# Sliding-window attention and a hardswish layer on one core: batch 0's q and k of pair 1 loaded as f32 by SP, pairs 2 and 3 two to an issue, and all of its V by POOL's casting queue

## The chip, the core and the metric

The kernel runs on one core of one Trainium2 chip. The core has TensorE (PE in the profile, with PEld for its weight loads), VectorE (DVE), ScalarE (ACT), GpSimd (POOL) and SyncE (SP), and 16 DMA engines that are shared by the queues of SP and POOL. The metric is the device time of one execution in microseconds, lower is better. Comparisons are made between runs on the same chip.

## What is computed

Attention over 8 batches, 8 heads, 576 positions and a head dimension of 64, in which each position sees itself and the 63 positions before it; then a two-matrix layer over the 4,608 tokens with a hardswish between:

```python
scores = scale * np.matmul(q, k.transpose(0, 1, 3, 2))
rel = pos[:, None] - pos[None, :]
mask = (rel >= 0) & (rel < 64)
scores = np.where(mask, scores, -1000000000.0)
attn = softmax(scores)                  # over the last axis
x = np.matmul(attn, v).transpose(0, 2, 1, 3).reshape(4608, 512)
h = x @ w_in                            # 512 -> 2048
g = h * np.clip(h + 3.0, 0.0, 6.0) / 6.0
out = g @ w_out                         # 2048 -> 512
```

Inputs and output are f32 in DRAM; the kernel computes on TensorE in bf16 with f32 sums.

## The kernel before

**Tiling.** Heads go in four pairs g = 0 to 3 (two heads of 64 fill 128 partitions). Queries go in blocks of 64; each sees 128 keys, and so V is kept in blocks of 128 rows in two alignments: blocks 0 to 3 (`NE = 4`) at multiples of 128, and blocks 4 to 7 shifted by 64 rows, which are made from the first four by copies with swapped partition halves (`shift_v`, line 428). The last 64 rows of each sequence ("e") have a block of their own. The layer works on 9 tiles of 512 tokens (`t`): 16 column chunks `fc` of the first matrix (`s1_part`, line 685), each finished by ACT (line 698) and DVE (line 703) into `gT`, then the second matrix (`s2_part`, line 724) for four groups `u` of 128 tokens.

**Batch 0.** Its attention has to be done before the first tile. q and k of a pair are loaded as 128 rows of nine positions (`A`), 2,304 bytes of f32 each, either as f32 by SP into `stage` and cast by ACT or DVE (`load_pair`, line 384), or cast to bf16 on the way by POOL's queue (`load_cast`, line 390). PE transposes them (`fold_pair`, line 490), ACT or DVE copy them out of PSUM (line 495), PE adds the mask and multiplies q by k (`scores`, lines 514 and 529), ACT takes the exponential (line 545). Then come V (line 574), the division by the row sums on DVE (lines 584 and 585), a transpose (line 600) and a copy into `xT`. In the kernel before, V of pairs 0 and 1 comes from SP: `load_tok` (line 395) loads one block of 128 rows and four heads at a time as f32, 512 packets of 256 bytes, and `cast_v` (line 440) casts each into both alignments. V of pairs 2 and 3 comes from POOL, one head at a time, in 512 packets that are cast to 128 bytes (`load_vhead`, line 415), and `shift_v` makes the second alignment.

**Order.** One list of operations is put in order by a planner (`Plan`, lines 47 to 209). It gives each operation an engine time and picks greedily, eight times over, so that the estimated DMA landings settle; operations with `alts` may go to any of several engines. What comes out is a fixed order for each engine: an engine then waits for whatever is late. The loads are kept in a chain (`then`), win and wout (the two matrices, in five and four loads) after batch 0's loads. For the first loads of each queue the planner does not estimate the landing but takes it from a list, in ns from its own start:

```python
LANDED = {
    "SP": (2970, 3660, 6210, 7840, 8150, 10350),
    "POOL": (4550, 6480, 7920, 9200, 10360, 10930, 11370, 11790, 12210, 12680),
}
```

After batch 0's loads POOL issues win, wout, q and k of batch 1 (two pairs in one issue), and V of batch 1 by rows; from batch 2 on q and k come by rows (`nq`, `nk`) and are transposed by DMA. PE alternates between the layer's tile t and the attention of batch t + 1. TensorE runs warm-up matmuls of ones (line 919) until its first real work.

Of the kernel before, what the change touches and what calls it, by code (L numbers as in the profile page):

```python
# [23 lines left out]
    "SP": (2970, 3660, 6210, 7840, 8150, 10350),  # L24
    "POOL": (4550, 6480, 7920, 9200, 10360, 10930, 11370, 11790, 12210, 12680),
# [187 lines left out]
def kernel(  # L213
# [14 lines left out]
    NG = H // 2  # L228
# [39 lines left out]
    NST = 2  # L268
# [115 lines left out]
    def load_pair(n, src, b, g, i, x):  # L384
        st = stage[i][:, x * R * D : (x + 1) * R * D]
        dma(P, 106, st, src[b, 2 * g : 2 * g + 2].rearrange("h (p j) d -> (h p) (j d)", j=R), writes=[("stp", n, g)])
        copy_op(R * D, A[n][:, g, :, :].rearrange("p j d -> p (j d)"), st, ("ACT", "DVE"),
                [("stp", n, g)], [("A", n, g)] + st_keys(i, 0, NG, range(KB)), sbuf=True, prio=700)
# [5 lines left out]

    def load_tok(src, b, i, g0, g1, kbs=tuple(range(KB))):
        st = stage[i][:].rearrange("p (k h d) -> p k h d", k=KB, h=H)
        hs = slice(2 * g0, 2 * g1)
        for kb in kbs:
            s0, ss = kb * P, min(P, S - kb * P)
            dma(ss * (g1 - g0) * 2, 18, st[:ss, kb, hs, :],  # L400
                src[b, hs, s0 : s0 + ss, :].rearrange("h s d -> s h d"),
                writes=st_keys(i, g0, g1, (kb,)))

    def load_heads(src, b, i, g):

        st = stage[i][:].rearrange("p (k h d) -> p k h d", k=KB, h=H)
        for h in range(2):
            dma(NE * P, 18, st[:, 0:NE, 2 * g + h, :], src[b, 2 * g + h, 0:MAIN, :].rearrange("(k s) d -> s k d", k=NE),
                writes=st_keys(i, g, g + 1, range(NE), (h,)))
        load_tok(src, b, i, g, g + 1, (NE,))  # L410

    def st_keys(i, g0, g1, kbs, hs=(0, 1)):
        return [("st", i, g, kb, h) for g in range(g0, g1) for kb in kbs for h in hs]
# [25 lines left out]

    def cast_v(i, g0, g1, engines, prio=0, after=(), parts=((0, NE), (NE, NE)), pieces=(0, 1, 2)):  # L440
        st = stage[i][:].rearrange("p (k g h d) -> p k g h d", k=KB, g=NG, h=2)
        gs = slice(g0, g1)
        vv = V[:, :, :, 0 : 3 * D].rearrange("p k g (t d) -> p k g t d", d=D)
        full, odd = parts
        for x, (rows, src, k0, (y, n)) in enumerate((
            (slice(0, P), slice(0, P), 0, full),
            (slice(0, D), slice(D, P), 0, odd),
            (slice(D, P), slice(0, D), 1, odd),
        )):
            if not n or x not in pieces:  # L450
                continue
            blks = range(y, y + n)
            k0 += y % NE
            copy_op(n * (g1 - g0) * P, vv[rows, y : y + n, gs, 0:3:2, :], st[src, k0 : k0 + n, gs, :, :], engines[x],
                    st_keys(i, g0, g1, range(k0, k0 + n)), [("V", g, x, blk) for g in range(g0, g1) for blk in blks],
                    sbuf=True, prio=prio, after=after)
# [353 lines left out]
    i0, iv = new_stage(), new_stage()  # L810
    load_pair("q", q, 0, 0, i0, 0)
    load_pair("k", k, 0, 0, i0, 1)
    load_tok(v, 0, iv, 0, 2, range(NE))
    then(load_cast("q", q, 0, 1, 2))
    then(load_cast("k", k, 0, 1, 2, after=chain))
    then(add("POOL", 600, lambda: make_identity(nc, ident32), writes=["c32"], after=chain))
    then(load_cast("q", q, 0, 2, 3, after=chain))
    then(load_cast("k", k, 0, 2, 3, after=chain))
    then(add("POOL", 900, mask_pool, writes=["m32"], after=chain))
    add("DVE", 550, far_mask, reads=["m32"], writes=["far"], prio=600)  # L820
    then(load_cast("q", q, 0, 3, 4, after=chain))
# [136 lines left out]
```

## Time and profile before

The kernel takes 303.85 us (median of 3 runs, 303.29 to 304.75). The profiled execution took 304.4 us.

| profiled execution | |
|---|---|
| time, span of the core's instructions | 304.4 us, 302.7 us |
| granted TensorE clock | 1.000 |
| PE, PEld busy | 289.8, 154.5 us |
| DVE, ACT, POOL busy | 199.6, 207.5, 127.1 us |
| DMA by POOL's queue (q0) | 98,896 packets, 17.80 MB |
| DMA by SP's queue (q1) | 38,832 packets, 18.42 MB |
| chain that ended last | PE 77%, DMA 10%, POOL 6%, issue 4% |

Times in the views are microseconds from the span's start. In the row of slices each digit is a fortieth of the span, in tenths of busy time. In the chain that ended last each line is start, length, what ran or was waited for. In the timeline each line is start, length, engine, line of the kernel, operation, output<-input, shape and count, and in brackets the idle time before it and what ended it. A DMA line of an engine is the issue alone; the transfer lands later. Bytes moved are counted as written.

### The profile page before, as it was taken

The numbers are of one execution on the slowest core, as the hardware profiler recorded it, in microseconds if no ns is written. First come the engines' busy times: TensorE is split into PE (matmuls) and PEld (weight loads), VectorE is DVE, ScalarE is ACT, GpSimd is POOL, SyncE is SP. The second block draws the span as 40 slices with busy tenths as digits, with TensorE's granted clock in tenths as the row PEclk, the third lists the DMA queues.
The fourth block names the chain that finished last, engine by engine and source line by source line (L and its number), as shares of the span: only waits on it lengthen the run. The fifth ranks groups of instructions, "written<-read, shape, count | busy, mean of one in ns | idle before, by whom it ended". The sixth has DMA issues, their size and how long they took to land.

```text
span 302.7 us, 6789 instructions
## 1 busy us (share of the span) xinstructions
PE 289.8 (96%) x2703; PEld 154.5 (51%) x2749; DVE 199.6 (66%) x326; ACT 207.5 (69%) x323; POOL 127.1 (42%) x178
## 2 busy tenths in 40 slices
PE   7799998999999999999999999999999999999996
PEld 6544554445544454445587554455445544444443
DVE  3659737686578795788777885778678767206700
ACT  4768846678778785878678767877687858217711
POOL 8874769409920990496089229803200000000000
DMA  8999999999998999999999989948900010011011
GB/s 169 194 209 205 205 185 111 109 193 89 166 115 183 99 144 151 177 128 90 204 178 120 135 162 175 128 90 163 141 2 35 36 69 3 35 69 37 0 69 69
DMA packets 137760, 36.65 MB, mean 121 GB/s; under 512 B 126337, under 2 KB 132993, under 8 KB 137729
## 3 DMA queue, kind: packets, MB, share of 16 engines
q0 software_dynamic: 98896, 17.80, 73.0%
q1 hardware_dynamic: 38832, 18.42, 24.7%
q8 instruction: 21, 0.34, 0.5%
q14 instruction: 11, 0.08, 0.1%
HBM read 36.70 MB, written 9.44 MB: 152 GB/s over the span
## 4 chain that ended last, share of the span: by engine, by line
PE 77%; DMA 10%; POOL 6%; issue 4%; DVE 1%; ACT 0%; SPq 0%; POOLq 0%; DVEq 0%
PE pn L724 33%; PE pn L685 15%; PE pa L685 12%; PE pb L685 8%; DMA Ak<-in_k_dram 7%; PE pa L626 4%; POOL nk L366 2%; DMA Tk<-nk 2%; DMA V<-in_v_dram 1%; PE pa L529 1%; POOL V L433 1%; PE pa L724 1%; POOL nq L366 1%; POOL V L366 1%; PE pb L626 1%
## 5 line engine op out<-in xcount | busy, mean ns | idle before, releaser
L724 PE MATMUL pn<-wout,gT 128*128 128x512 bf16 x532 | 125.2, 379 | 2.1 <-issue 1.1
L685 PEld LDWEIGHTS <-win 128*128 128x128 bf16 x640 | 61.9, 98 | 60.8 <-issue 0.3
L724 PEld LDWEIGHTS <-gT 128*128 128x128 bf16 x592 | 54.1, 98 | 57.5
L685 PE MATMUL pn<-xT,win 128*128 128x512 bf16 (+1 forms) x274 | 63.2, 358 | 0.4
L703 DVE SCALAR_TENSOR_TENSOR gT<-t,pn 128x512 bf16<-128x512 bf16 x63 | 43.1, 686 | 11.1 <-ACT t L698 10.9
L698 ACT ACTIVATE t<-pn,half 128x512 bf16<-128x512 f32 x63 | 43.3, 689 | 9.9 <-PE pn L685 9.4
L685 PE MATMUL pa<-xT,win 128*128 128x512 bf16 (+1 forms) x202 | 48.0, 358 | 0.3
L703 DVE SCALAR_TENSOR_TENSOR gT<-t,pa 128x512 bf16<-128x512 bf16 x47 | 32.1, 687 | 23.7 <-ACT t L698 23.4
L366 POOL DMA_DIRECT2D nk<-in_k_dram x60 | 45.9, 812 | 1.2 <-DMA Ak<-in_k_dram 0.7
L698 ACT ACTIVATE t<-pa,half 128x512 bf16<-128x512 f32 x47 | 32.1, 687 | 8.6 <-PE pa L685 8.1
L646 DVE TENSOR_TENSOR xT<-pa,rec 64x512 bf16<-64x512 f32 (+1 forms) x48 | 32.5, 677 | 6.7 <-ACT rec L635 5.7
L685 PE MATMUL pb<-xT,win 128*128 128x512 bf16 (+1 forms) x149 | 35.3, 357 | 0.5 <-issue 0.5
L366 POOL DMA_DIRECT2D V<-in_v_dram x40 | 33.2, 853 | 4.7 <-PE pa L529 1.2
L703 DVE SCALAR_TENSOR_TENSOR gT<-t,pb 128x512 bf16<-128x512 bf16 x34 | 23.3, 687 | 16.3 <-ACT t L698 16.3
L737 ACT COPY osb<-pn 128x512 f32<-128x512 f32 x18 | 10.5, 585 | 33.5 <-PE pn L724 33.5
L632 ACT ACTIVATE rec<-pa 64x512 f32<-64x512 f32 (+1 forms) x48 | 27.9, 582 | 5.2 <-PE pa L626 4.1
L801 POOL COPY scrap<-Tk 128x1 bf16<-128x1 bf16 x6 | 1.1, 188 | 69.5 <-DMA Tk<-nk 69.5
L698 ACT ACTIVATE t<-pb,half 128x512 bf16<-128x512 f32 x34 | 23.4, 689 | 7.7 <-PE pb L685 7.7
L366 POOL DMA_DIRECT2D nq<-in_q_dram x30 | 27.6, 920 | 2.4 <-DMA wout<-in_moe_w_out_dram 1.6
L545 ACT ACTIVATE pT<-pa 128x1024 bf16<-128x1024 f32 x24 | 23.6, 1020 | 0.5 <-PE pa L529 0.5
L626 PEld LDWEIGHTS <-V 128*128 128x128 bf16 x464 | 17.5, 98 | 8.8 <-DVE xT L646 1.5
L554 DVE TENSOR_TENSOR pT<-pT,mask 128x1024 bf16<-128x1024 bf16 x28 | 19.1, 698 | 4.1 <-ACT pT L545 4.0
(88 smaller groups left out, 210.0 us busy)
## 6 DMA issues: line engine op xcount, KB each, us to landing
out_dram<-osb SPq DMA_DIRECT2D x35, 256.0 KB, 2.5
V<-in_v_dram POOLq DMA_DIRECT2D x28, 128.0 KB, 4.3
nq<-in_q_dram POOLq DMA_DIRECT2D x24, 128.0 KB, 4.1
nk<-in_k_dram POOLq DMA_DIRECT2D x48, 64.0 KB, 3.9
wout<-in_moe_w_out_dram POOLq DMA_DIRECT2D x4, 512.0 KB, 14.8
win<-in_moe_w_in_dram POOLq DMA_DIRECT2D x3, 512.0 KB, 9.8
V<-in_v_dram POOLq DMA_DIRECT2D x12, 64.0 KB, 5.6
Aq<-in_q_dram POOLq DMA_DIRECT2D x2, 288.0 KB, 14.0
```

The source lines that it names most:

```text
L366: em = lambda: e.dma_start(out=out_ap, in_=in_ap)
L433: alts = {e: (c, (lambda e=e, rows=rows, src=src, k0=k0, n=n: cpy(e)(out=vv[rows, NE : NE + n, gs, 0:3:2, :], in_=vv[src, k0 : k0 + n, gs, ...
L545: nc.scalar.activation(out=p_[:].rearrange("p j h c -> p h j c"), in_=wide(add_far if masked else op, name)[:, :, 0 : n * D].rearrange("p ...
L554: nc.vector.tensor_tensor(out=pp, in0=pp, in1=mask[:, m0 : m0 + n, :, :].rearrange("p j h c -> p (j h c)"), op=MULT)
L626: nc.tensor.matmul(wide(op, name)[:, h, y * D : (y + 1) * D], lhsT=V[:, blk, g, h * D : h * D + P], rhs=p_[:, y, h, :], start=True, stop=True)
L632: add("ACT", act(n), lambda h=h: nc.scalar.activation(out=rc[rows[h], 0:n], in_=wide(op, name)[rows[1 - h], h, 0:n], func=LN), reads=[key] ...
L646: nc.vector.tensor_tensor(out=o, in0=a, in1=z, op=MULT)
L685: nc.tensor.matmul(bank(op, name)[:, to : to + n], lhsT=win16[:, g, fc * P : (fc + 1) * P], rhs=xT[:, g, o : o + n], start=(g == 0), stop= ...
L698: nc.scalar.activation(out=t1[ti][:], in_=bank(op, name), func=RELU, bias=half[:], scale=1.0 / 6.0)
L703: nc.vector.scalar_tensor_tensor(out=gT[:, fc, :], in0=t1[ti][:], scalar=1.0, in1=bank(op, name), op0=MIN, op1=MULT)
L724: nc.tensor.matmul(bank(op, name)[:, 0:n], lhsT=gT[:, fc, col : col + P], rhs=wout16[:, fc, js], start=(fc == 0), stop=(fc == NFC - 1))
L737: alts = {e: (f(n), (lambda e=e: cpy(e)(out=osb[oi][:, js], in_=bank(op, name)[:, 0:n])), False) for e, f in (("DVE", dve), ("ACT", act))}
```

## The change

V of all four pairs is loaded by POOL, head by head, with `load_vhead`, and gets its second alignment by `shift_v`. `load_tok`, `cast_v` and two functions that go with them are removed, also the late cast of V's last block. q and k of pairs 0 and 1 are loaded as f32 by SP with `load_pair`, in the order q0, k0, q1, k1; q and k of pairs 2 and 3 are loaded by POOL in one issue each, 256 packets instead of 128. One staging buffer goes. The planner's list has four landings for SP and ten for POOL, with new values.

```diff
 LANDED = {
-    "SP": (2970, 3660, 6210, 7840, 8150, 10350),
-    "POOL": (4550, 6480, 7920, 9200, 10360, 10930, 11370, 11790, 12210, 12680),
+    "SP": (2900, 3700, 5400, 7100),
+    "POOL": (7100, 8900, 9350, 9800, 10250, 10700, 11150, 11600, 12050, 12500),
 }
...
-    NST = 2
+    NST = 1
...
         copy_op(R * D, A[n][:, g, :, :].rearrange("p j d -> p (j d)"), st, ("ACT", "DVE"),
-                [("stp", n, g)], [("A", n, g)] + st_keys(i, 0, NG, range(KB)), sbuf=True, prio=700)
+                [("stp", n, g)], [("A", n, g)], sbuf=True, prio=700)
...
-    i0, iv = new_stage(), new_stage()
-    load_pair("q", q, 0, 0, i0, 0)
-    load_pair("k", k, 0, 0, i0, 1)
-    load_tok(v, 0, iv, 0, 2, range(NE))
-    then(load_cast("q", q, 0, 1, 2))
-    then(load_cast("k", k, 0, 1, 2, after=chain))
+    i0 = new_stage()
+    for g in range(2):
+        load_pair("q", q, 0, g, i0, 2 * g)
+        load_pair("k", k, 0, g, i0, 2 * g + 1)
+    then(load_cast("q", q, 0, 2, 4))
+    then(load_cast("k", k, 0, 2, 4, after=chain))
     then(add("POOL", 600, lambda: make_identity(nc, ident32), writes=["c32"], after=chain))
-    then(load_cast("q", q, 0, 2, 3, after=chain))
-    then(load_cast("k", k, 0, 2, 3, after=chain))
     then(add("POOL", 900, mask_pool, writes=["m32"], after=chain))
     add("DVE", 550, far_mask, reads=["m32"], writes=["far"], prio=600)
-    then(load_cast("q", q, 0, 3, 4, after=chain))
-    then(load_cast("k", k, 0, 3, 4, after=chain))
-    for g in range(2, NG):
+    for g in range(NG):
         for h in range(2):
             then(load_vhead(0, g, h, chain)).prio = 3000
...
-    NOW, REST = ((0, NE), (NE, NE - 1)), ((0, 0), (2 * NE - 1, 1))
-    for parts in ((0, 2), (NE, 1)), ((2, 2), (NE + 1, 2)):
-        cast_v(iv, 0, 2, (THREE,) * 3, prio=700, parts=parts)
     for a, z in ((0, 2), (2, 4), (4, 8), (8, 12), (12, 16)):
         then(load_win(a, z, after=chain)).prio = 2000 if z <= 8 else 0
-    for g in range(2, NG):
+    for g in range(NG):
         shift_v(g, g + 1, THREE, 700)
...
-                cast_v(iv, 0, 2, (THREE,) * 3, parts=REST, prio=-2500, pieces=(1,))
```

More of the change, by code (lines that the diff above doesn't have):

```diff
@@ L393, in load_cast @@
                    writes=[("A", n, g) for g in range(g0, g1)], eng="POOL", after=after)
[L395 to L413, printed above, removed]
     def load_vhead(b, g, h, after=()):
@@ L438, in shift_v @@
                 stream="copy" if len(engines) > 1 else engines[0])
[L440 to L456, printed above, removed]
     V_PARTS = [(0, blk) for blk in range(NE)] + [(x, NE + blk) for x in (1, 2) for blk in range(NE - 1)]
```

## Prediction

> **What bounds the kernel now.** I read the page first (engine shares, the 40 slices), then the chain that ended last in order of time, then the timeline of the first 60 us, the DMA issues with their times to landing, and last the PE waits. Page:
>
> ```profile
> PE 289.8 (96%) x2703; PEld 154.5 (51%) x2749; DVE 199.6 (66%) x326; ACT 207.5 (69%) x323; POOL 127.1 (42%) x178
> PE   7799998999999999999999999999999999999996
> DMA  8999999999998999999999989948900010011011
> ```
>
> PE is full from the third slice on, and the DMA engines are full beside it for 28 of 40 slices. An early gain must therefore be asked twice: does PE start its main work sooner, and does the data of batch 1 come sooner? The chain in order of time answers:
>
> ```profile
> 5.53 6.77 DMA Ak<-in_k_dram
> ...
> 21.15 1.08 PE pa L685 x5
> ...
> 27.96 13.26 DMA Ak<-in_k_dram
> 41.51 0.74 POOL nk L366
> ...
> 46.35 1.41 POOL V L433 x2
> ...
> 100.86 4.40 DMA V<-in_v_dram
> ```
>
> Up to 12.3 us the chain is batch 0's last k; a short PE stretch follows; then from 28 to 50 us it runs over batch 1's k, POOL's issues and POOL's copies of V, and it touches DMA again up to 105 us. From there it is PE alone. In the timeline:
>
> ```profile
> 9.62 0.74 POOL L366 DMA_DIRECT2D win<-in_moe_w_in_dram  x1 [0.58 <-DMA Aq<-in_q_dram]
> ...
> 17.34 0.60 PE L685 MATMUL pn<-xT,win 128*128 128x512 bf16 x2
> ...
> 41.27 0.36 PEld L490 LDWEIGHTS <-Ak 64*64 64x64 bf16 x18
> ...
> 44.75 0.29 DVE L433 COPY V<-V 64x512 bf16<-64x512 bf16 x1 [0.34 <-DMA V<-in_v_dram]
> ...
> 50.19 0.38 PE L574 MATMUL pb<-V,pT 128*64 128x65 bf16 x12 [0.83 <-POOL V L433]
> ```
>
> The MoE matmuls begin at 17.34. Batch 1's k lands at 41.23 (issue 27.96 plus 13.3) and is folded at 41.27; its V lands at 44.62 and is copied at 44.75: both without slack, so batch 1 goes at the pace of the DMA queue. POOL's eleventh load (the first above) waits for its third: Aq, issued at 3.08, lands 6.3 later at 9.34, and win goes out at 9.62. The next three repeat it (landings 10.30, 11.21, 12.30; issues 10.58, 11.49, 12.58): each POOL load waits for the landing of the eighth before it, and 0.28 us more.
>
> **The change part by part.** *DMA time of batch 0.* Rates come from stretches in which one kind fills the engines:
>
> ```profile
> DMA packets 211, 0.45 MB, mean 300 GB/s; under 512 B 16, under 2 KB 16, under 8 KB 211
> ...
> DMA packets 225, 0.22 MB, mean 219 GB/s; under 512 B 56, under 2 KB 224, under 8 KB 224
> ...
> DMA packets 1176, 0.15 MB, mean 153 GB/s; under 512 B 1161, under 2 KB 1176, under 8 KB 1176
> ```
>
> These are 2.0 to 3.5 us (195 f32 rows of 2,304 B by SP: 130 per us), 9.5 to 10.5 (168 cast rows beside some small ones: about 170 per us) and 11.5 to 12.5 (about 1,165 V packets by POOL per us). SP's V packets reached 411 in half a us beside 23 cast rows (7.0 to 7.5): at least 820 per us, at most about 1,150 when the casts are taken off. Before: 256/130 + 768/170 + 2048/1165 + 2048/(820 to 1150) = 2.0 + 4.5 + 1.8 + (1.8 to 2.5) = 10.1 to 10.8 us. After: 512/130 + 512/170 + 4096/1165 = 3.9 + 3.0 + 3.5 = 10.4 us. So the sum alone gives between -0.4 and +0.3. The first SP packet comes at 1.8 and the last V lands at 13.88, so before also holds some 1 us of poor filling between 4 and 6 us, when POOL's queue has just started and SP's is on small packets (151 GB/s from 4 to 6, after 290 in the 2 us before), and a tail. With four row loads SP's queue stays full until about 8 us, so up to 0.7 of this can go. I take -0.3, with -0.8 and +0.5 as ends.
>
> A rule of the Trainium skill (DMA: Bandwidth & Descriptors, Issuing engines are not separate DMA queues) says that DMAs from all queues run on the same 16 engines and interleave, so that moving them saves issue time alone; by it this term would be 0 and the time 0.3 us longer. The trace agrees so far: both queues together moved 232 GB/s (6 to 9 us), between 300 for SP alone and 219 for POOL nearly alone.
>
> *POOL's queue.* Removed: six row issues (0.54 to 0.69 us); added: two wider ones (0.71, as at 17.91) and four V issues (0.77). Sum: -3.6 + 1.4 + 3.1 = +0.9 us. It hides while the DMA engines have a backlog. The eighth V load (V7) is now POOL's tenth and waits for its second, k of pairs 2 and 3. All 1,024 row packets are through at about 1.8 + 3.9 + 3.0 + 0.3 = 9.0 us, plus 0.7 to land, 9.7; V7 goes out at 10.0, and its first packet comes 1.6 to 2.3 later (V at 68.43: 1.6; the first Aq: 2.3), 11.6 to 12.3. The engines reach V7 at 9.0 + 7 x 0.44 = 12.1. So it just fits: 0, at most 0.2. The win load behind it waits for V's first head (about 10.1), goes out at 10.7 and begins at 12.3 to 13.0 against V's end at 12.5: 0 to 0.5, taken as 0.1.
>
> *Copies.* Removed: seven casts of V (two on ACT, 0.61; five on DVE, 0.29 to 0.42). Added: two casts of rows (0.46 and 0.51, as at 3.72 and 5.28) and four shifts (0.28 on DVE to 0.62 on ACT or POOL). 2.9 us go and 2.1 to 3.5 come, spread over engines busy for 57% (DVE) and 71% (ACT) of the time from 4 to 16 us: 0 on the path, cover gone +0.6.
>
> Against V on POOL speaks a rule of the skill (SBUF — State Buffer, SBUF: two separate sides): a copy f32 to bf16 on DVE locks POOL out of writing descriptors. The row first: POOL's issue at 3.63, beside DVE's cast at 3.72, took 0.66 against 0.54 to 0.56 for its neighbours, so 0.1 for each cast, and two more casts add 0.2, under the backlog. By the rule two whole casts, 1.0 us, would be added, still under the backlog; the row disagrees with a full block.
>
> *The head on PE.* Scores of pairs 2 and 3 need rows that landed at 9.34 to 12.30 and now at about 8.0 and 9.7; pair 1's come later (8.2 against 7.40). The exponentials (four of 1.02 on ACT), the last at 15.05, can end 2 us sooner. V arrives pair by pair from 10.1 to 13.2; after its last shift (0.3 to 0.6), PV 0.45, normalisation 0.90, turn 0.40 and copy 0.58 give about 16.4 for the last x instead of 18.96. The first matmuls then need win, landing at 15.23, 16.57 and 19.80 before: fc 0 to 3 can be done by 19, and fc 4, at 21.42 now, goes at 19.8 + 0.2. So PE gains up to 1.4 us at fc 4.
>
> *Where that goes.* Next late is wout: its fourth load lands at 38.39, and the 21st matmul of line 724, the first to need it, is at 39.29, so 0.9 is the most that survives; then k at 41.23 and V at 44.62, with no slack. PE has only tile 0's second stage to fill in until batch 1's attention is done (last x at 55.9), so a lead turns into a longer wait (0.83 at 49.35). I keep 0.2 of 1.4; the ends are 0 and 1.4.
>
> *The order after the head* is worked out anew from the planner's list of landings. It can lose the waits of 0.83 (49.35) and 0.67 (76.91) or add as many: -1.5 to +1.5, taken as 0.
>
> Sum: -0.3 + 0.1 + 0 - 0.2 = -0.4 us on the profiled execution's 304.4 (span 302.7 and 1.7 around it), 304.0. That execution lies 0.55 above the median 303.85, so I expect **303.5 us**: no change. Half a per cent (1.5 us) is about what a measurement of this kernel can tell from none.
>
> **The rivals.** *The lead is kept (faster).* If the new order fills the wait at 49 us by moving batch 1's V copies off POOL, the 1.4 stays, the DMA gives 0.3 to 0.8 and the 0.83 wait goes: 303.85 - 2.2 = 301.6, and up to 300.9. For it: POOL alone copies V from 46.35 to 51.4 while ACT and DVE have gaps. Against it: V lands at 44.62 whatever the head does, and PE idles only 1.9 us from 17.5 to 56, so there is little to win.
>
> *The eight-deep queue bites (slower).* If k of pairs 2 and 3 lands after about 10.0 us, V7 begins after the engines have run dry, and V's end, win's landings and each load behind them come later by the same amount, into k and V of batch 1 that have no slack. What decides is how the engines share packets between the queues: an Aq of the old kernel took 6.3 us to land beside SP's small packets, and two in one issue could take 9.5, landing at 11.5. Then V7 is 1.6 to 1.8 us late: 303.85 + 1.7 = 305.6, to 306 with win's 0.5. For it: the four 0.28 us steps. Against: 1,024 packets at the measured rates are through at 9.0.
>
> *The new order is worse (slower).* Two more waits like 0.83 and 0.67 on POOL's copies, and the same gains: 303.5 + 1.5 to 2.5 = about 305.5. For it: PE and SP follow a fixed order, and every landing in the old list of the planner is earlier than the trace's by 0.7 to 2.0 us. Against: the new list is of the same kind.
>
> **How the numbers follow.** No change 0.59; lead kept 0.15; queue bites 0.14; worse order 0.12. Faster 0.15, same 0.59, slower 0.26. The likeliest is 303.5, its own range by the ends 302.4 to 305.2. The range of eight in ten reaches into the rivals on both sides: 302.2 to 305.7.
>
> **What would show it.** Right: the last V of batch 0 lands at 13.2 to 13.9, POOL's win loads go out from 10.4 to 11.0, the first matmul of line 685 is at 15 to 16.5 and fc 4 near 20, but batch 1's k lands within 0.8 us of 41.2 and the first matmuls of tile 1 are within 1 us of 55.4, with PE's waits between 38 and 52 us grown. Wrong towards faster: tile 1 begins before 54. Wrong towards slower: k of pairs 2 and 3 lands after 10.5, or a gap in the DMA row between 11 and 14 us, and win (4 to 8) after 21.

## The result and the profile after

The changed kernel takes **306.55 us** (median of 7 runs, 304.19 to 308.04) against 303.85: a ratio of **1.0074 [1.0051, 1.0097]**, 0.74% or 2.25 us (the two medians as they stand differ by 2.70), so slower by more than the half per cent that a measurement can tell from no change. The forecast of 303.5 [302.2, 305.7] does not hold it. The profiled execution took 305.44 us with a span of 303.7, 1.0 more than before; the 7 runs spread over 3.9 us.

The page, with the lines that answer to those of before (line numbers behind L390 are now smaller by up to 38: L413 is `shift_v`, L452 the fold, L536 the product with V, L647 the first matrix, L686 the second; L366 is still the DMA issue, L343 the copies):

```profile
PE 293.9 (97%) x2748; PEld 155.0 (51%) x2748; DVE 199.7 (66%) x326; ACT 207.4 (68%) x322; POOL 128.5 (42%) x178
PE   6889898999999999999999999999999999999995
PEclk9799999999999999999999999999999999999999
DMA  7999999999999999799999989948900010011011
```

PE is not idler. Its busy time is longer by 4.1 us, but with 45 more records than before, so that says little. New is the second digit of the clock row, a stretch at half clock that before did not have (granted clock 1.000 over the whole span, now 0.994). The chain that ended last, in order of time:

```profile
2.14 8.64 DMA Ak<-in_k_dram
10.78 0.28 issue
11.06 0.74 POOL V L366
11.80 1.68 POOL win L366 x3
...
16.65 12.94 DMA wout<-in_moe_w_out_dram
...
30.12 13.27 DMA Ak<-in_k_dram
...
48.00 1.41 POOL V L413 x2
```

It still begins with batch 0's last k, and that transfer now takes 8.64 us and is followed by POOL's issue of V and win, and then by wout, where the old chain had PE. From batch 1's k on the steps of the old chain are there, later: the k is issued at 30.12 instead of 27.96, and V is copied from 48.00 instead of 46.35. POOL's timeline of the head, and PE's (its first line is that of the kernel before, for the same q):

```profile
9.45 0.92 POOL L366 DMA_DIRECT2D V<-in_v_dram  x1 [0.58 <-DMA Aq<-in_q_dram]
11.06 0.74 POOL L366 DMA_DIRECT2D V<-in_v_dram  x1 [0.70 <-DMA Ak<-in_k_dram]
11.79 2.23 POOL L366 DMA_DIRECT2D win<-in_moe_w_in_dram  x3
...
15.19 1.49 POOL L366 DMA_DIRECT2D win<-in_moe_w_in_dram  x2
```

```profile
6.49 0.47 PE L490 MATMUL pb<-fold,Aq 64*64 64x64 bf16 x18 [0.17 <-DMA Aq<-in_q_dram]
```

```profile
8.61 0.69 PE L452 MATMUL pb<-fold,Aq 64*64 64x64 bf16 x18 [1.67 <-DVE Aq L343]
...
18.12 0.59 PE L647 MATMUL pn<-xT,win 128*128 128x512 bf16 x2
```

The last two V heads (the last is the forecast's V7) wait for q and k of pairs 2 and 3, and win goes out behind them, at 11.79 to 15.19 instead of being under way. PE waits 1.67 us for pair 1's q (0.17 before) and starts the MoE matmuls at 18.12 instead of 17.34. What the DMA engines did in that time, before and then after (stretch, its length, busy time and instructions of PE, PEld, DVE, ACT and POOL, granted clock, DMA share, GB/s):

```profile
12.00:14.00 2.00, 1.50 (x47) 1.00 (x39) 1.18 (x3) 1.58 (x3) 1.58 (x3) 1.00 1.81 180
16.00:18.50 2.50, 2.18 (x36) 1.33 (x33) 2.07 (x6) 1.82 (x5) 2.46 (x5) 1.00 1.25 207
```

```profile
8.00:10.00 2.00, 1.39 (x48) 1.35 (x50) 0.86 (x3) 0.65 (x2) 1.42 (x3) 0.52 1.55 196
12.00:14.00 2.00, 2.00 (x64) 1.18 (x56) 1.55 (x5) 1.82 (x3) 2.00 (x3) 1.00 1.44 90
16.00:18.50 2.50, 1.80 (x45) 1.15 (x42) 2.37 (x7) 1.47 (x4) 2.46 (x5) 1.00 1.03 124
```

From 12 to 14 us they move 90 GB/s instead of 180, and from 16 to 18.5 they move 124 instead of 207: POOL's queue runs low, and the bytes are made up later. The landings show how the loss travels:

| lands (us of the span) | before | forecast | after |
|---|---|---|---|
| pair 1's k | 7.40 | 8.2 | 9.58 (its q 8.07) |
| k of pairs 2, 3 (before: of pair 3) | 12.30 | 9.7 | 10.78 |
| last V of batch 0 | 13.88 | 13.2 to 13.9 | 14.30 |
| win, chunks 4 to 7 | 19.80 | unmoved | 21.94 |
| fourth wout | 38.39 | – | 40.49 |
| batch 1's last k by `load_cast` | 41.23 | 41.2 ± 0.8 | 43.38 |
| batch 1's V | 44.62 | no slack | 46.79 |

From win on, everything is 2.1 to 2.2 us late. The time lost in this execution is smaller; the likely reason is that PE has other work to put in. The first matmuls of tile 1 are 1.64 us late, those of tile 2 are 1.51 late, and those of tiles 3 to 8 are 0.94 late, since the last short waits of before (0.43 us together, at 105 us) are gone.

### The profile page after: what moved, and what is told of

Read it like the earlier page. It is cut to its first block, busy times and chain, and to the rows that moved or that the text cites. A ratio compares the mean times of both kernels' runs of the same rounds, so it can differ in the third digit from the quotient of the medians.

```text
span 303.7 us, 6828 instructions
## 1 busy us (share of the span) xinstructions
PE 293.9 (97%) x2748; PEld 155.0 (51%) x2748; DVE 199.7 (66%) x326; ACT 207.4 (68%) x322; POOL 128.5 (42%) x178
## 4 chain that ended last, share of the span: by engine, by line
PE 79%; DMA 11%; POOL 6%; issue 2%; ACT 0%; POOLq 0%
PE pn L686 35%; PE pn L647 16%; PE pa L647 12%; PE pb L647 9%; DMA Ak<-in_k_dram 7%; DMA wout<-in_moe_w_out_dram 4%; PE pa L588 3%; PE pa L491 2%; POOL nk L366 2%; POOL V L413 2%; PE pa L686 1%; POOL nq L366 1%; POOL win L366 1%; PE pb L588 1%; POOL V L366 1%
## 5 line engine op out<-in xcount | busy, mean ns | idle before, releaser
L686 PE MATMUL pn<-wout,gT 128*128 128x512 bf16 x560 | 129.5, 379 | 0.0
L647 PEld LDWEIGHTS <-win 128*128 128x128 bf16 x640 | 61.8, 98 | 60.8 <-DMA win<-in_moe_w_in_dram 0.3
L686 PEld LDWEIGHTS <-gT 128*128 128x128 bf16 x592 | 54.2, 98 | 57.4
L647 PE MATMUL pn<-xT,win 128*128 128x512 bf16 (+1 forms) x280 | 63.6, 358 | 0.0
L665 DVE SCALAR_TENSOR_TENSOR gT<-t,pn 128x512 bf16<-128x512 bf16 x63 | 43.1, 686 | 11.5 <-ACT t L660 11.2
L647 PE MATMUL pa<-xT,win 128*128 128x512 bf16 (+1 forms) x208 | 48.5, 359 | 0.0
L366 POOL DMA_DIRECT2D nk<-in_k_dram x60 | 46.0, 816 | 0.7 <-DMA Ak<-in_k_dram 0.6
L366 POOL DMA_DIRECT2D V<-in_v_dram x44 | 36.4, 845 | 5.0 <-issue 1.4
L647 PE MATMUL pb<-xT,win 128*128 128x512 bf16 (+1 forms) x152 | 36.0, 357 | 0.0
L366 POOL DMA_DIRECT2D nq<-in_q_dram x30 | 27.7, 924 | 2.5 <-DMA wout<-in_moe_w_out_dram 2.2
L507 ACT ACTIVATE pT<-pa 128x1024 bf16<-128x1024 f32 x25 | 24.7, 1022 | 0.8 <-PE pa L491 0.8
L516 DVE TENSOR_TENSOR pT<-pT,mask 128x1024 bf16<-128x1024 bf16 x28 | 19.2, 699 | 4.1 <-ACT pT L507 4.0
```

The source lines that it names most:

```text
L366: em = lambda: e.dma_start(out=out_ap, in_=in_ap)
L507: nc.scalar.activation(out=p_[:].rearrange("p j h c -> p h j c"), in_=wide(add_far if masked else op, name)[:, :, 0 : n * D].rearrange("p ...
L516: nc.vector.tensor_tensor(out=pp, in0=pp, in1=mask[:, m0 : m0 + n, :, :].rearrange("p j h c -> p (j h c)"), op=MULT)
L647: nc.tensor.matmul(bank(op, name)[:, to : to + n], lhsT=win16[:, g, fc * P : (fc + 1) * P], rhs=xT[:, g, o : o + n], start=(g == 0), stop= ...
L665: nc.vector.scalar_tensor_tensor(out=gT[:, fc, :], in0=t1[ti][:], scalar=1.0, in1=bank(op, name), op0=MIN, op1=MULT)
L686: nc.tensor.matmul(bank(op, name)[:, 0:n], lhsT=gT[:, fc, col : col + P], rhs=wout16[:, fc, js], start=(fc == 0), stop=(fc == NFC - 1))
```

## The experiments

Every kernel below computes the whole reference. A ratio is to the kernel before, in runs on the same chip in the same batch of runs; batches ran on different chips. The changed kernel itself is in the first three batches, and no ratio is compared across batches without saying so.

### Is it the clock, the rows, or V?

First batch. Three candidates: the half clock after PE's 1.67 us wait; the rows (q and k); V by POOL. The changed kernel again:

> The changed kernel again, as the control for the others on the same chip. All theories: about 305 to 307, slower than the kernel before by 0.5 to 1%. Clock theory: the granted clock over the span differs from run to run (0.994 or 0.988, as in the first seven runs), and the time goes with it, about 1.0 to 1.8 us for each 0.006; a run at 1.000 is within 0.5 us of the kernel before. Queue theory: win (chunks 4 to 7) lands near 22 and k of batch 1 near 43.4 whatever the clock does, and a run at 1.000 is slower too, by 1 to 2 us.

307.45 us, 1.0106 [1.0051, 1.0160]. Its profiled execution (308.34 us) is an extreme case of the same thing: k of pairs 2 and 3 landed at 13.34 and V7 was issued at 13.62. From 12 to 14 us of this run the DMA engines move 54 GB/s, from 14 to 16 us 43:

```profile
12.00:14.00 2.00, 1.64 (x43) 1.10 (x38) 1.44 (x3) 0.64 (x1) 0.38 (x1) 0.50 0.89 54
```

**The clock.** 40 matmuls of ones fill PE's wait for pair 1's q:

```diff
+            if op.alloc == (("F", "q", 0, 1),):
+                for _ in range(40):
+                    warm(op)
             op.emit()
```

> The changed kernel with 40 warm-up matmuls of ones (96 columns) on PE ahead of the transposes of pair 1's q, in the wait of 1.67 us that ends at 8.61; nothing else differs. Clock theory: the granted clock is 1.000 in every run, the transposes of pair 1 take 0.47 us and not 0.69, and the time falls to 303.9 to 304.5, the spread of the runs with it. Queue theory: the DMA landings stay (k of pairs 2 and 3 at 10.8, win 4 to 7 near 22) and the time stays within 0.5 us of the changed kernel's. Both together: about half of the loss comes back.

307.1 us, 1.0102 [1.0072, 1.0132]: nothing gained. In the profiled execution the granted clock was 1.000, and PE's timeline shows that the edit did what it should:

```profile
7.07 1.87 PE L873 MATMUL pb<-ones 128*128 128x96 bf16 x40
9.63 0.47 PE L452 MATMUL pb<-fold,Aq 64*64 64x64 bf16 x18 [0.69 <-DVE Aq L343]
```

The fold takes 0.47 instead of 0.69 us, and the time is that of the changed kernel. POOL's timeline says why:

```profile
12.06 0.74 POOL L366 DMA_DIRECT2D V<-in_v_dram  x1 [0.99 <-DMA Ak<-in_k_dram]
12.79 2.24 POOL L366 DMA_DIRECT2D win<-in_moe_w_in_dram  x3
```

V7 and win still wait for k (landed at 11.77). In the second batch (another chip) the changed kernel's k landed at 11.77 too, with half clock from 10.3 to 13.7 us: 306.41 us there, 306.49 here without it. The half clock in the head is real, and no cost of it shows there; as the cause of the loss the theory falls. (The first seven runs had suggested it, with 304.19 us at a clock of 1.000 and 308.04 at 0.989. In the third batch the changed kernel took 305.87 at 1.000 and between 305.10 and 306.37 at 0.989.)

**One half alone.** The rows part alone, as a change of the kernel before, keeps V as it was (SP loads pairs 0 and 1 of it, now behind four rows); the list of landings follows:

```diff
     load_pair("q", q, 0, 0, i0, 0)
     load_pair("k", k, 0, 0, i0, 1)
+    load_pair("q", q, 0, 1, i0, 2)
+    load_pair("k", k, 0, 1, i0, 3)
     load_tok(v, 0, iv, 0, 2, range(NE))
-    then(load_cast("q", q, 0, 1, 2))
-    then(load_cast("k", k, 0, 1, 2, after=chain))
+    then(load_cast("q", q, 0, 2, 4))
+    then(load_cast("k", k, 0, 2, 4, after=chain))
...
-    then(load_cast("q", q, 0, 2, 3, after=chain))
-    then(load_cast("k", k, 0, 2, 3, after=chain))
...
-    then(load_cast("q", q, 0, 3, 4, after=chain))
-    then(load_cast("k", k, 0, 3, 4, after=chain))
```

The V part alone keeps all loads of q and k as before, and loads all of V by head:

```diff
-    load_tok(v, 0, iv, 0, 2, range(NE))
...
-    for g in range(2, NG):
+    for g in range(NG):
         for h in range(2):
             then(load_vhead(0, g, h, chain)).prio = 3000
...
-    for parts in ((0, 2), (NE, 1)), ((2, 2), (NE + 1, 2)):
-        cast_v(iv, 0, 2, (THREE,) * 3, prio=700, parts=parts)
...
-    for g in range(2, NG):
+    for g in range(NG):
         shift_v(g, g + 1, THREE, 700)
```

> One part alone: rows of q and k as in the changed kernel (pair 1 as f32 by SP, pairs 2 and 3 in one issue each by POOL), V as in the kernel before (pairs 0 and 1 by SP in small packets, behind the rows, pairs 2 and 3 by POOL). POOL's eighth load is then win 2 to 3, so that win waits for less. Clock theory: pair 1's q lands near 8 again, PE waits over 1.5 us before it, the clock drops, and it is slower than before by 0.3 to 1%. Queue theory: POOL's loads go out early, win 4 to 7 lands by 20.5, and the time is within 0.3% of the kernel before unless V by SP (now behind the rows) lands after 14.

> The other part alone: V of all pairs by POOL, rows as in the kernel before (pair 0 by SP, pairs 1 to 3 by POOL one to an issue), so 14 loads by POOL ahead of win. Pair 1's q lands near 5.5 to 6.5. Clock theory: no PE wait over 1 us in the head, clock 1.000, time within 0.3% of the kernel before. Queue theory: win waits still longer for its place, the rings run dry before it, win 4 to 7 lands at 22 or later, and the time is 0.5 to 1% over the kernel before.

Rows alone: 307.96 us, 1.0125 [1.0061, 1.0190]. SP's V now stands behind four large rows and lands at 16.51, POOL's at 16.60, the wide k at 11.99. V alone: 306.00 us, 1.0062 [1.0032, 1.0092], although its rows were all in by 9.92. The two halves do not add up to the whole; each loses by itself, the rows part with SP's V pushed back, which the whole change does not have. What happens with V alone, its POOL timeline and windows show:

```profile
6.34 5.96 POOL L366 DMA_DIRECT2D V<-in_v_dram  x8
```

```profile
11.00:13.50 2.50, 1.02 (x34) 0.77 (x36) 2.29 (x6) 0.99 (x2) 2.50 (x4) 1.00 1.40 87
```

Eight issues back to back take 5.96 us, 0.75 each for 512 packets of 128 bytes written, and the DMA engines move 87 GB/s behind them. The 1,165 packets per us (0.44 us for a head) of the forecast were measured while a backlog was drained; without one, POOL's issuing sets the pace. win therefore goes out at 12.21 and chunks 4 to 7 land at 21.85, nearly the 21.94 of the changed kernel, by another way. This execution also had half clock from 14.8 to 21.6 us, over the layer's first matmuls (from 17.89), but the two of its ten runs at a clock of 1.000 took 306.17 and 305.95 us, no less than the median.

### Is it the depth of POOL's queue, or the order?

Second batch. V comes in four loads of 1,024 packets (a block of 128 rows, all heads) instead of eight of 512; once on the changed kernel, where that makes six loads ahead of win, so that V waits for no earlier landing, and once with the rows as before, as a change of V alone. The lists of landings follow. A third kernel (second diff) changes only the planner's list, to the landings measured in the changed kernel less 0.73 us, so that the order on PE fits what comes.

```diff
-    for g in range(NG):
-        for h in range(2):
-            then(load_vhead(0, g, h, chain)).prio = 3000
+    for blk in range(NE):
+        then(load_vrows(0, blk, chain)).prio = 3000
```

```diff
-    "SP": (2900, 3700, 5400, 7100),
-    "POOL": (7100, 8900, 9350, 9800, 10250, 10700, 11150, 11600, 12050, 12500),
+    "SP": (2980, 3850, 7340, 8850),
+    "POOL": (8430, 10050, 10510, 10930, 11990, 12160, 12340, 12690, 13140, 13570),
```

> The changed kernel once more, as the control on this chip. All theories: 305 to 308, with k of pairs 2 and 3 landing between 10.5 and 13.5 and win 4 to 7 between 21.9 and 23.6.

> The changed kernel with V of batch 0 in four loads by POOL instead of eight (one block of 128 rows and all heads each, 1,024 packets, as batch 1 does), and the planner's list of landings set near the measured ones. POOL then has six loads ahead of win, so that V and the first two win loads wait for no landing, and each V load writes 1,024 packets in 0.88 us where a head wrote 512 in 0.77. Queue theory: no stretch under 130 GB/s between 9 and 20 us, V landed by 13.3, win 4 to 7 by 20.5, k of batch 1 by 42, and the time within 0.3% of the kernel before, that is 303.3 to 304.8. Rows theory (the shared rows land late and that alone sets the head): k of pairs 2 and 3 at 10.8 or later, the scores of pairs 1 to 3 late, and the time stays 0.6 to 1% over the kernel before although win lands early. Clock theory is already down; a granted clock under 1 would still show as 1 to 1.7 us.

> Rows of q and k as in the kernel before (pair 0 by SP, pairs 1 to 3 by POOL one to an issue), V of all pairs by POOL in four loads of a block each, the planner's list set to the landings measured for these rows. Ten loads by POOL ahead of win, and the first eleven places free by 7 us. Queue theory: rows land by 10, V by 13, win 4 to 7 by 20, and the time is 302.5 to 304.0, at or under the kernel before; against the part with eight heads (306.0) it gains 2 to 3 us. Rows theory: the same, as the rows are not shared. If it stays near 306, neither the queue's depth nor its issue rate is what V by POOL costs.

> The changed kernel with only the planner's list of landings changed, to the values that its own trace showed (less 0.73 us for the planner's start), so that the order of work on the engines is worked out for what happens. Order theory (the new order is wrong because the list was too early): at least 1 us comes back, 304 to 305.5. Queue theory: the landings stay, and with them the time, 305 to 307.5, within 0.5 us of the control.

| kernel | median us | ratio | k of pairs 2, 3 | last V | win 4 to 7 |
|---|---|---|---|---|---|
| changed | 306.20 | 1.0059 [1.0028, 1.0089] | 11.77 | 15.31 | 22.80 |
| changed, V in blocks | 306.07 | 1.0052 [1.0014, 1.0089] | 13.07 | 16.48 | 21.69 |
| rows as before, V in blocks | 305.08 | 1.0044 [1.0024, 1.0064] | 10.72 (pair 3's) | 15.46 | 20.03 |
| changed, list only | 305.52 | 1.0044 [1.0015, 1.0073] | 9.42 | 13.26 | 19.78 |

*Blocks on the changed kernel.* In the windows of this run the gap in the transfers is gone, and PE is without work instead:

```profile
8.00:10.00 2.00, 0.00 (x0) 0.00 (x0) 0.13 (x1) 0.00 (x0) 1.43 (x3) 0.68 1.36 202
12.00:14.00 2.00, 0.92 (x21) 0.69 (x20) 1.13 (x2) 0.44 (x2) 0.64 (x1) 0.50 1.98 175
```

The DMA engines move 175 GB/s, but k lands at 13.07 and pair 1's k at 12.58, PE does nothing from 8 to 10 us, and nothing is won. V's packets run beside the rows (3,391 of 4,096 were through before the last row packet), but so they do in the changed kernel (2,848 in this batch), and that blocks make the rows later is not shown: the same rows landed at 13.34 in the first batch without them. The held-back issue is gone for V alone. It now falls on win, whose third and fourth loads wait for q and k:

```profile
9.95 0.75 POOL L366 DMA_DIRECT2D win<-in_moe_w_in_dram  x1 [0.57 <-DMA Aq<-in_q_dram]
13.36 1.59 POOL L366 DMA_DIRECT2D win<-in_moe_w_in_dram  x2 [2.66 <-DMA Ak<-in_k_dram]
```

So freeing V's issues does not help while the rows are late.

*Blocks with the rows as before* have the lowest median of the batch (305.08, where 302.5 to 304.0 was expected). But a block brings all heads at once and the last one is needed for every pair; on PE's timeline:

```profile
16.25 1.00 PE L574 MATMUL pa<-V,pT 128*64 128x65 bf16 x27 [3.36 <-POOL V L433]
```

win is only 0.2 us late there. What the trace shows in its place is this wait of PE for V's shifted copy, and matmuls at half clock from 16.7 to 23.5 us; what each costs is not told apart.

*The list alone* has the same loads as the changed kernel. Its profiled execution was the fastest of its 10 runs, 302.66 us, and there k of pairs 2 and 3 landed at 9.42, V7 went out at 9.71 and win 4 to 7 landed at 19.78: the landings of the forecast (9.7, 10.0, unmoved), and a time below its 304.0. The other nine runs lie from 303.18 to 306.43, and the median's gain of 0.68 us on the changed kernel is within the intervals. So the forecast's landings can occur; the times of the other runs suggest that they are not the usual ones.

### Does the landing of that k set the time?

By now three profiled executions of one and the same program showed that landing at three times. In the view of DMA issues, the line for k of pairs 2 and 3 (last column: us from issue, at 2.14, to landing), first run, then the first and second batch's:

```profile
Ak<-in_k_dram POOLq DMA_DIRECT2D x1, 288.0 KB, 8.6
```

```profile
Ak<-in_k_dram POOLq DMA_DIRECT2D x1, 288.0 KB, 11.2
```

```profile
Ak<-in_k_dram POOLq DMA_DIRECT2D x1, 288.0 KB, 9.6
```

Landing at 10.78, 13.34 and 11.77 went with 305.44, 308.34 and 306.41 us: the line through the first two has (308.34 - 305.44) / (13.34 - 10.78) = 1.13 us per us. For the third batch it was written down ahead that a fourth execution would lie on it, and POOL's two row issues were moved behind the identity and the masks, so that SP's four rows have the DMA engines nearly to themselves (58 of their 512 packets were left when POOL's first row packet came, against 298 in the changed kernel):

```diff
-    then(load_cast("q", q, 0, 2, 4))
-    then(load_cast("k", k, 0, 2, 4, after=chain))
-    then(add("POOL", 600, lambda: make_identity(nc, ident32), writes=["c32"], after=chain))
+    then(add("POOL", 600, lambda: make_identity(nc, ident32), writes=["c32"]))
     then(add("POOL", 900, mask_pool, writes=["m32"], after=chain))
+    then(add("POOL", 1300, mask_pool16, reads=["m32"], writes=["mask"], after=chain))
+    then(load_cast("q", q, 0, 2, 4, after=chain))
+    then(load_cast("k", k, 0, 2, 4, after=chain))
```

The list follows, and `mask_pool16` (1.2 us of POOL, at 18.2 in the changed kernel) leaves its old place behind wout, where POOL's next critical issue, k at 30.12, waits for a landing anyway. The second kernel of this batch adds V in blocks.

> The changed kernel as the control on this chip, and one more point for time against landing. Tail theory (the rows that two queues load at once end late on the slowest of the 16 DMA engines, and the time follows that tail): the profiled execution lies within 0.5 us of the line through the three so far, 305.44 + 1.13 for each us that k of pairs 2 and 3 lands after 10.78.

> The changed kernel with the same loads, but POOL makes the identity and both masks before it issues q and k of pairs 2 and 3 (near 3.5 us and not at 1.3), so that SP's four row loads are nearly through before POOL's begin; the planner's list follows. Tail theory: pair 1's q lands before 6 and its k before 7, k of pairs 2 and 3 by 10.3 with its tail short, PE has no wait over 1.2 us in the head, the granted clock is 1.000 or 0.994, and the time falls by 1.5 to 3 us against the control, to 303 to 304.5. Queue theory (what costs is that V's last load and win wait for places of POOL's queue): k of pairs 2 and 3 is still what V's last load waits for, so not over 0.7 us better than the control. If k of pairs 2 and 3 still lands after 11, two rows in one issue are late by themselves, and not by sharing.

> As the one before it, with V by POOL in four loads of a block of rows (1,024 packets, all heads) instead of eight heads, so that the queue holds six loads ahead of win and V is not bound by POOL's 0.77 us for 512 packets. Tail theory with issue bound: rows as in the one before, V landed by 13.3, win 4 to 7 by 19.8, and the time 302.5 to 304.0 if PE's wait for the last block stays under 1.6 us; with a longer wait the half clock falls on the first matmuls of the layer and costs 1 to 2 us. Queue theory: better than the one before it by 1 us or more.

| kernel | median us | ratio | k of pairs 2, 3 | last V | win 4 to 7 |
|---|---|---|---|---|---|
| before | 303.92 | 1 | – | – | – |
| changed | 306.05 | 1.0061 [1.0040, 1.0081] | 11.19 | 14.70 | 21.66 |
| rows not shared | 305.32 | 1.0043 [1.0021, 1.0065] | 9.69 | 13.59 | 21.16 |
| rows not shared, V in blocks | 304.58 | 1.0018 [0.9997, 1.0040] | 10.24 | 14.15 | 19.62 |

The line gives 305.44 + 1.13 x (11.19 - 10.78) = 305.90 for the changed kernel's profiled execution; it took 305.87, at a clock of 1.000. The warm-up kernel's execution of the first batch, with the same loads, fits too (landing 11.77: 306.56 by the line, 306.49 measured). The list-only kernel's does not: at 9.42 the line gives 303.90, and it took 302.66. These are few executions on several chips, and the landing was observed in them, not set.

In the kernel with rows not shared it was set. k is issued 1.8 us later (3.96) and lands 1.5 us earlier; in the view of DMA issues of that kernel:

```profile
Ak<-in_k_dram POOLq DMA_DIRECT2D x1, 288.0 KB, 5.7
```

Pair 1's q lands at 6.06 instead of 9.08. The median is 0.73 us lower. That is less than the 1.5 to 3 us written down ahead and than the 1.13 x 1.5 = 1.7 of the line, and the two intervals overlap widely (1.0040 to 1.0081 and 1.0021 to 1.0065), so by itself it is not told from nothing. The line is thus no price of the landing. One place where a gain can go is in this trace: PE waits 1.97 us at 74.4 us, where the kernel before waited 0.67 at 76.91.

```profile
76.36 0.63 PE L588 MATMUL pa<-pT,V 128*128 128x64 bf16 x16 [1.97 <-ACT p L507]
```

In the head, V by head is left, on POOL's timeline and in the windows:

```profile
4.67 6.05 POOL L366 DMA_DIRECT2D V<-in_v_dram  x8
10.70 0.76 POOL L366 DMA_DIRECT2D win<-in_moe_w_in_dram  x1
11.99 1.49 POOL L366 DMA_DIRECT2D win<-in_moe_w_in_dram  x2 [0.53 <-DMA V<-in_v_dram]
```

```profile
16.00:18.00 2.00, 1.54 (x15) 0.68 (x12) 1.32 (x3) 1.32 (x3) 2.00 (x4) 1.00 1.14 151
```

Eight issues of V take 6.05 us, win's second load waits for V's first landing, and the engines move 151 GB/s. With blocks, the same two views:

```profile
4.67 3.78 POOL L366 DMA_DIRECT2D V<-in_v_dram  x4
8.42 3.75 POOL L366 DMA_DIRECT2D win<-in_moe_w_in_dram  x5
```

```profile
16.00:18.00 2.00, 1.30 (x36) 0.97 (x35) 1.90 (x6) 0.87 (x3) 2.00 (x4) 1.00 1.25 208
```

All of win is issued by 12.2, the engines move 208 GB/s, and win 4 to 7 lands at 19.62, slightly earlier than before the change. The median is another 0.74 us lower, although V in blocks makes the head itself late (the first MoE matmul at 19.2, against 16.8 with V by head). Of the 2.13 us between the medians of the changed kernel and the one before in this batch (306.05 - 303.92), the two edits together gave 1.47 (1.0061 [1.0040, 1.0081] against 1.0018 [0.9997, 1.0040]); 0.66 are left, with an interval that includes nothing.

### The rest: clock or order?

The nearest kernel still had half clock in two stretches of its head (9 to 12.5 and 19.3 to 22.7 us). Eight warm-up matmuls at each of 14 places of batch 0's attention keep the clock up:

```diff
+            if op.eng == "PE" and op.alloc and (
+                (op.alloc[0][0] == "F" and op.alloc[0][2] == 0 and op.alloc[0][3] > 0)
+                or (op.alloc[0][0] in "OX" and op.alloc[0][1] == 0 and op.alloc[0][2] != "e")
+            ):
+                for _ in range(8):
+                    warm(op)
             op.emit()
```

> The version with POOL's rows behind SP's and V in four blocks (304.58, ratio 1.0018), and eight warm-up matmuls (0.3 us at full clock) on PE ahead of each transpose of pairs 1 to 3's rows, each of batch 0's products with V and each of their turns: 14 places, most of them waits of 0.2 to 0.6 us. Clock theory, for what is left of the loss: the granted clock is 1.000 in most runs, the half clock from 19.3 to 22.7 us, which fell on the layer's first matmuls, is gone, and the time falls by 0.8 to 1.7 us to 302.9 to 303.8, at or under the kernel before. Other theory (what is left is the new order and later data for batch 1): the clock is 1.000 and the time stays within 0.4 us of 304.6, or rises by the added matmuls.

306.97 us, 1.0110 [1.0085, 1.0136], at a clock of 0.993 to 1.000 (1.000 in the profiled execution). This batch is on another chip than the 1.0018. The first MoE matmul is at 21.8, against 19.2 in the kernel without them and 17.34 before the change, so the added matmuls seem to lie on the path themselves. This doesn't tell what the half clock costs in that place; it shows only that it is not bought back in this way.

Last, the two kernels of the third batch with their planner's list set near the landings measured in them there, nothing else (V in blocks, then V by head), on yet another chip:

```diff
-    "SP": (2980, 3850, 4500, 5200),
-    "POOL": (7300, 9000, 9900, 10800, 11700, 12600),
+    "SP": (2980, 3880, 5880, 6650),
+    "POOL": (8080, 9510, 10370, 11890, 12590, 13420),
```

```diff
-    "SP": (2980, 3850, 4500, 5200),
-    "POOL": (7300, 9000, 9450, 9900, 10350, 10800, 11250, 11700, 12150, 12600),
+    "SP": (2980, 3730, 5330, 6110),
+    "POOL": (7510, 8960, 9410, 10980, 11150, 11320, 11560, 12030, 12450, 12860),
```

> The version with POOL's rows behind SP's and V in four blocks (304.58, ratio 1.0018), with only the planner's list of landings changed to those that its trace showed, less 0.73 us. Order theory (the rest of the loss is an order of work made for landings that are 0.3 to 1.0 us too early): 303.3 to 304.1, ratio 0.996 to 1.000. Data theory (the rest is V and its last tail): within 0.3 us of 304.6, ratio 1.001 to 1.003.

> The version with POOL's rows behind SP's and V by heads (305.32, ratio 1.0043), with only the planner's list changed to the landings that its trace showed, less 0.73 us. Order theory: 304.0 to 304.8, ratio 1.000 to 1.003, and PE's wait of 1.97 us at 74 us gone. Data theory: within 0.3 us of 305.3, ratio 1.003 to 1.006; V's heads still hold back win, which lands (chunks 4 to 7) near 21.

V in blocks with its list at the landings: 306.35 us, 1.0092 [1.0075, 1.0109]; V by head: 305.81, 1.0082 [1.0057, 1.0107]. Both lie above the ranges written down for either theory (at most 1.003 and 1.006). On this chip k of pairs 2 and 3 landed at 10.74 and 10.91 in the profiled executions, later than the 10.24 and 9.69 of the same loads in the third batch to which the lists were set. So the lists were too early again, by 0.5 and 1.2 us for this k, and these two kernels don't tell whether the order is the rest of the loss. PE's wait of 1.97 us did not go either: 1.48 at 75.1 us with V by head. In the second batch the list alone did move the medians from 306.20 to 305.52, within the intervals of the two. **Open** stays where the last 0.66 us go, and why the ratios of these two are above those of the third batch: the order, the chip and the spread of the landing are not told apart by these runs. With that it is also open how far the gain of 1.47 us holds on another chip. No version that beats the kernel before was found.

## Why the prediction was wrong

**The step that failed** is "All 1,024 row packets are through at about 1.8 + 3.9 + 3.0 + 0.3 = 9.0 us, plus 0.7 to land, 9.7; V7 goes out at 10.0 [...] So it just fits: 0". The bulk was near the sum, by which 90% of the row packets would be through at 1.8 + 0.9 x 6.9 + 0.3 = 8.3 us: they were at 8.9. But a load has landed when its last packet has, and the last came at 10.5; in the first two batches' executions 90% were through at 9.3 and 8.1, and the last at 12.5 and 11.5. Nor did V wait for the rows to end, as the sum had it. From 8.9 us to the last row packet the changed kernel's DMA engines moved 86 row packets and, beside them, 1,337 of under 512 bytes, nearly all of V:

```profile
DMA packets 1423, 0.27 MB, mean 164 GB/s; under 512 B 1337, under 2 KB 1421, under 8 KB 1423
```

So k landed at 10.78, and in other executions at 11.19, 11.77 and 13.34. Dividing packets by a mean rate gives the time at which the engines on the whole are done; a landing is that of the slowest part. V7 then went out at 11.06 instead of 10.0, win behind it, and all later landings came 2.1 to 2.2 us late: the term taken as 0 to 0.2 was this. How much of the 2.25 us of time it costs is not settled. The line through the executions puts the forecast's 9.7 at 305.44 - 1.13 x 1.08 = 304.2, close to the 304.0 that I had summed, and the list-only kernel took 302.66 with k at 9.42. But with the rows not shared k landed at 9.69 and the time was still 305.52. The kernel before has a smaller tail (90% at 10.4, last at 11.8).

The Trainium skill (DMA: Bandwidth & Descriptors, Why a DMA increments its semaphore by 16 and not by 1) says that a DMA runs on up to 16 engines that finish independently, and that only the full count means that all has landed. The tails agree with it; the trace doesn't keep the 16 engines apart, so no run here shows that it is one engine that is late.

**The second step that failed** is POOL's "+0.9 us. It hides while the DMA engines have a backlog". The backlog of V was gone at about 12 us (536 packets in the half us before it, 364 in the one after), and 512 packets of V cost POOL 0.75 us of issuing against the 0.44 at which I had the engines eat them. I had priced the issue rightly (0.77) and then let the engines, not POOL, set the pace. V alone (1.0062) and, with the rows not shared, V in blocks (0.74 us by the medians) point to it; neither edit changed the issuing alone.

**The rival that came true** is the eight-deep queue, in its place and near its price: it decided "after about 10.0 us", k landed at 10.78, and V7 was issued 0.28 behind it at 11.06, the step that the old trace showed four times. It gave 305.6 to 306 and had 0.14; measured 306.55. Its condition, how the engines share packets between the queues, was named, and I set it aside by the very mean rate that failed. Its mechanism is not the whole matter, though: V alone lost 0.62% with its rows in by 9.92 and no load of V held back, and with V in blocks and the rows still shared the time stayed (1.0052 against 1.0059).

**Right** were: where a shift of the DMA queue ends (batch 1's k and V "both without slack": both came 2.15 us later, the same as win); the direction for pair 1, which comes later (though at 9.58, not 8.2); the DMA sum, as far as it can be seen (where k landed at 9.42, the last V landed at 13.26 against 13.88 before; the forecast was -0.3); and two sign posts for "slower" (k after 10.5, win after 21). The third, a gap in the DMA row between 11 and 14 us, showed in the first execution only as 90 GB/s instead of 180, and in the one with 308.34 us as 54.

**Not seen ahead**: PE's head wait of 1.67 us for pair 1's q, with half a clock after it. No cost of it shows in the runs. The lead of up to 1.4 us at fc 4 did not arise, since V and win came later, not sooner.

**The new order** moved waits but cost little: PE's waits of 0.83 and 0.67 us became 0.83 (51.00) and 0.52 (78.56), and those at 105 us went. My 0 for it stands within the ±1.5 given for this kernel; other orders had a wait of up to 1.97 us there. One reading behind that rival was wrong: not every landing of the old list is 0.7 to 2.0 us earlier than the trace's, since two of SP's loads of V landed at 8.07 and 8.52 against 7.84 and 8.15 in the list.

The Trainium skill (DMA: Bandwidth & Descriptors, Issuing engines are not separate DMA queues), weighed in the forecast, says that DMAs of all queues run on the same 16 engines, so that moving them saves issue time alone. The result agrees in that nothing was gained by moving rows to SP; the 0.3 us by which the forecast would then have been longer is not enough either.

The Trainium skill (SBUF — State Buffer, SBUF: two separate sides), weighed too, says that a copy of f32 on DVE locks POOL out of writing descriptors. The changed trace has one more row on it: POOL's issue at 9.45, beside DVE's cast of 0.46 us at 9.60, took 0.92 us against 0.74 for the one after it, so 0.2 more and not the whole cast. In the second batch an issue at 10.54 beside such a cast at 10.48 took 0.75. No part of the loss is traced to it here.

## What to carry to other kernels

A mean packet rate gives the time at which the DMA engines are done on average; a load that something waits for needs the time of its last packet, taken from a comparable load in the trace, with its spread over several executions; a line through a few executions is not the price of that landing until an edit has set it. Before putting more loads on a queue with a limited number outstanding, find which landing releases the next issue, and whether the issuing engine can feed the DMA engines when the backlog is gone: loads with more packets to an issue (here 1,024 in 0.89 to 0.94 us instead of 512 in 0.75) are the cheaper form. Where two queues' large loads are wanted one after the other, issuing the second later can make both land earlier (here 1.8 us later and, in one pair of executions, 1.5 us earlier). Over the five kernels with the later issue pair 1's q landed at 5.7 to 6.6 us and k of pairs 2 and 3 at 9.7 to 11.0; in the four executions of the changed kernel it was 8.1 to 9.9 and 10.8 to 13.3, and in the list-only kernel 6.6 and 9.4.

## What the runs showed of the hardware

- **Landing spread.** The same wide row load (256 packets of 2,304 bytes read, beside 512 rows of SP and 256 of POOL) landed 8.6, 9.0, 9.6 and 11.2 us after its issue in four executions of one program, and 7.3 in a fifth with the same loads in another order on PE. In each of the four, one or two packets of POOL's queue that started at 3.7 to 5.7 us of the span, just after that queue had begun, took 1.2 to 2.2 us (the longest, 2.20, in the run with the landing after 11.2); in the fifth none took over 1 us. With rows not shared there was none where that load landed 5.7 and 6.3 us after its issue, and one to three of 1.1 to 1.5 us where it took 6.8 to 7.0. Of the 1,024 row packets, 4 to 13 took over 0.5 us in the four executions. What makes these long isn't settled, nor that they cause the tail.
- **Sharing.** Issued with SP's four rows nearly through, the same load took 5.7 to 7.0 us in five kernels.
- **Clock.** The granted clock was 0.5 for one to three stretches of 3.4 us each (8.1 to 11.5 in the changed kernel behind the wait of 1.67 us, 16.7 to 23.5 behind the wait of 3.36 us above). The Trainium skill (TensorE: Matmul & The Clock Gate, Part 1: The HAM clock gate) says that the clock is set by windows of about 3.4 us in which PE's activity is watched, and halved after an idle one; the length agrees. The length of a wait alone did not decide it here: the changed kernel's execution of the third batch had a wait of 1.76 us at a clock of 1.000, and with rows not shared and V in blocks two such stretches (9.1 to 12.5 and 19.3 to 22.7) came with no wait in the head over 0.6 us.
